# A ring of six one-chunk buffers for r, k, v, shared with w2, and w1 loaded in 12 KB runs

## Chip, cores, metric

One core of one Trainium2 chip. The metric is device microseconds of one execution. The kernel before: 128.2 us, median of 3 runs (128.12 to 129.5). Runs more than 1.5% above the fastest run of the same kernel are called slow; ratios use fast runs alone.

## The reference, cut to what matters

```python
# r, k, v: (4, 8, 768, 48) f32; w, u: (8, 48)
for t in range(S):                                   # linear attention, per batch and head
    cur = einsum('bhd,bhe->bhde', u * k[t], v[t])
    y[t] = einsum('bhd,bhde->bhe', r[t], state + cur)
    state = w * state + einsum('bhd,bhe->bhde', k[t], v[t])
x = y as (3072, 384)
# soft mixture of experts: 8 experts of 4 slots, w1: (8, 384, 1024), w2: (8, 1024, 384) f32
logits = x @ phi
slot_input = softmax(logits, axis=0).T @ x
slot_out[e] = relu(slot_input[e] @ w1[e]) @ w2[e]
out = softmax(logits, axis=1) @ slot_out             # (3072, 384) f32
```

Inputs are 14.2 MB of r, k, v and 25.2 MB of weights. The weights are cast to bf16 on the way in, 12.6 MB written.

## The kernel before, where it matters

The attention runs in 12 chunks of 256 rows (`nS` = 12). r, k, v come through SyncE's hardware queue (q1 in the profile), the weights through GpSimd's software queue (q0). GpSimd also does three multiplies of every chunk but the first. Three terms are used below: the masks are VectorE's multiplies of the attention scores, two groups per iteration; an expert is one 768 KB weight load of w1 or w2; the second down projection is the product with w2 of the last four experts, after which the output follows.

```python
ld = ctx.enter_context(tc.tile_pool(name="ld", bufs=2))      # two buffers of one batch (3 chunks)
SRC = ((1, k), (0, r), (2, v))
def load_part(bt, i):                 # batch 0: chunk by chunk, 384 B reads
    for x, src in SRC:
        nc.sync.dma_start(out=bt[:, x, :, i, :],
                          in_=src[0, :, i * TS:(i + 1) * TS, :].rearrange("h (p j) d -> p h (j d)", j=J))
def load(b):                          # batches 1 to 3: three chunks in one load, built as 1536 B reads
    bt = new_batch(b)
    for x, src in SRC:
        nc.sync.dma_start(out=bt[:, x].rearrange("p h i m -> p (h i) m"),
                          in_=src[b].rearrange("h (i p j) d -> p (h i) (j d)", p=P, j=J))
# ... cut ...
w1_ap = moe_w1.rearrange("e (mo p) f -> p e mo f", p=P)      # three 4 KB runs per partition and expert
# ... cut: mults(n) for n > 0 ...
    nc.gpsimd.tensor_mul(rr[:, :, :, 0:D], r_l, W_n[:])      # waits for r of chunk n
    load_w(inner)                                            # issues weights in between
    nc.gpsimd.tensor_mul(kk[:, :, :, 0:D], k_l, W_k[:])      # waits for k of chunk n
    nc.gpsimd.tensor_mul(ku, ku, u_b)
# ... cut: schedule, experts issued inside mults(n + 3) and at the end of iteration n ...
W_IN = [0, 0, 1, 0, 0, 1, 1, 1, 1]
W_AT = [0, 0, 1, 0, 0, 1, 1, 1, 3, 0, 0]
mults(1); mults(2); load_w(2)
for n in range(nS - 1):
    masks(n, 0)                                              # VectorE, start of iteration n
    if n + 3 < nS: mults(n + 3, W_IN[n])
    # ... cut ...
    if n % nSb == 1: load(n // nSb + 2)                      # next batch, when its buffer is read out
    load_w(W_AT[n])                                          # after n = 8: all the rest
```

The last four experts of w2 go into one batch buffer once r, k, v have left it (`w_tail`).

The softmax here doesn't subtract the row's maximum and nothing guards it: scores larger than these inputs give would overflow.

## Time and profile before

| | before |
|---|---|
| time, span of the profiled run | 128.2 us, 126.4 us |
| last masks (end of the attention's VectorE work) | 92.04 us |
| second down projection waits for w2 until | 104.93 us |
| from there to the end | 21.5 us |

The prediction shows the slices and the chain; three more readings are needed later. First, the page's rows for GpSimd (busy share) and the granted TensorE clock (share of full speed), 40 slices of 3.16 us, in tenths:

```profile
POOL 6009999799999799999999999992420000055100
PEclk9999999999959999977999599958999999995555
```

GpSimd is busy almost without a gap from 10 us to about 84.

Third, all the waits of the list of waits that r, k, v cause (total us, times, longest):

```profile
POOL rr L254 <- DMA rkv<-in_r_dram: 8.7, 3, 6.8
...
ACT v_bf L264 <- DMA rkv<-in_v_dram: 1.8, 1, 1.8
...
DVE rkv L283 <- POOL rkv L257: 1.1, 1, 1.1
```

6.8 of the 8.7 us are the first wait, for the first loads to land.

### The profile page before, as it was taken

The numbers are of one execution on the slowest core, as the hardware profiler recorded it, in microseconds if no ns is written. First come the engines' busy times: TensorE is split into PE (matmuls) and PEld (weight loads), VectorE is DVE, ScalarE is ACT, GpSimd is POOL, SyncE is SP. The second block draws the span as 40 slices with busy tenths as digits, with TensorE's granted clock in tenths as the row PEclk, the third lists the DMA queues.
The fourth block names the chain that finished last, engine by engine and source line by source line (L and its number), as shares of the span: only waits on it lengthen the run. The fifth ranks groups of instructions, "written<-read, shape, count | busy, mean of one in ns | idle before, by whom it ended". The sixth has DMA issues, their size and how long they took to land.

```text
span 126.4 us, 4165 instructions
## 1 busy us (share of the span) xinstructions
PE 97.5 (77%) x1783; PEld 70.5 (56%) x1783; DVE 91.7 (73%) x181; ACT 78.4 (62%) x144; POOL 81.4 (64%) x77
## 2 busy tenths in 40 slices
PE   3994898887599969189798969799999998793000
PEld 3493575665487757177576657677665565520000
DVE  5599989969989999578999798979762411497000
ACT  5869498868479968488597688886431510495000
POOL 6009999799999799999999999992420000055100
PEclk9999999999959999977999599958999999995555
DMA  3999998999999999999999999999999998079992
GB/s 84 299 325 325 335 327 264 321 208 251 265 332 267 235 259 270 340 289 270 258 255 252 226 211 223 221 214 215 210 218 212 218 199 160 2 264 372 381 403 81
DMA packets 23080, 31.78 MB, mean 251 GB/s; under 512 B 10451, under 2 KB 18005, under 8 KB 23061
## 3 DMA queue, kind: packets, MB, share of 16 engines
q0 software_dynamic: 5360, 15.19, 56.7%
q1 hardware_dynamic: 17280, 16.32, 41.8%
q8 instruction: 14, 0.23, 0.7%
q10 hardware_dynamic: 420, 0.00, 0.2%
q14 instruction: 6, 0.04, 0.1%
HBM read 39.38 MB, written 4.72 MB: 349 GB/s over the span
## 4 chain that ended last, share of the span: by engine, by line
POOL 33%; DMA 25%; PE 10%; SPq 9%; DVE 8%; issue 4%; ACT 2%; POOLq 1%; DVEq 0%
DMA w_tail<-in_moe_w_dram 16%; POOL kk L256 10%; POOL rkv L257 9%; DMA rkv<-in_r_dram 8%; SPq L75 7%; POOL rr L254 7%; DVE o_s L748 5%; POOL w_all L187 2%; POOL w_h L194 2%; PE t_p L312 2%; POOL hT L121 1%; SPq L83 1%; PE so_p L681 1%; PE sr_p L712 1%; PE aat_p L331 1%
## 5 line engine op out<-in xcount | busy, mean ns | idle before, releaser
L343 DVE TENSOR_TENSOR at_s<-aat_p,mask 128x512 bf16<-128x512 f32 x47 | 30.2, 684 | 4.0 <-PE aat_p L331 3.8
L254 POOL TENSOR_TENSOR rr<-rkv,W_n 128x768 bf16<-128x768 f32 x11 | 19.9, 1813 | 8.9 <-DMA rkv<-in_r_dram 8.7
L257 POOL TENSOR_TENSOR rkv<-rkv,u_rep 128x768 f32<-128x768 f32 x11 | 19.9, 1812 | 0.9
L256 POOL TENSOR_TENSOR kk<-rkv,W_k 128x768 bf16<-128x768 f32 x11 | 20.0, 1817 | 0.1
L331 PE MATMUL aat_p<-t_rr,t_kk 64*64 64x128 bf16 x376 | 12.1, 243 | 7.8 <-ACT t_kk L319 4.7
L277 ACT COPY rpun<-rkv 128x384 f32<-128x384 f32 x23 | 11.3, 490 | 10.3 <-PE rpun L491 8.2
L331 PEld LDWEIGHTS <-t_kk 64*64 64x64 bf16 x384 | 8.6, 119 | 11.2 <-ACT t_kk L319 6.9
L283 DVE TENSOR_TENSOR rkv<-rkv,rpun 128x384 f32<-128x384 f32 x23 | 12.6, 546 | 1.3 <-POOL rkv L257 1.1
L301 DVE TENSOR_TENSOR dv<-v_bf,rpun 128x768 bf16<-128x768 bf16 x12 | 11.4, 953 | 2.4 <-ACT v_bf L264 1.4
L319 ACT COPY t_kk<-t_p 128x1024 bf16<-128x1024 bf16 x12 | 12.2, 1014 | 1.0 <-PE t_p L312 1.0
L752 POOL DMA_DIRECT2D out_dram<-o_s x1 | 0.6, 552 | 18.4 <-ACT o_s L750 18.4
L294 DVE TENSOR_REDUCE rpun<-rkv 128x16 f32<-128x768 f32 x12 | 11.5, 961 | 0.4
L382 PE MATMUL s_p<-v_bf,kk 64*128 64x96 bf16 x160 | 11.8, 222 | 0.0
L319 ACT COPY t_rr<-t_p 128x1024 bf16<-128x1024 bf16 x11 | 11.2, 1016 | 0.5 <-PE t_p L312 0.3
L391 DVE TENSOR_TENSOR st<-s_p,wm 128x384 bf16<-128x384 f32 x20 | 10.9, 546 | 0.4 <-PE s_p L382 0.4
L264 ACT CAST v_bf<-rkv 128x768 bf16<-128x768 f32 x12 | 10.0, 830 | 1.8 <-DMA rkv<-in_v_dram 1.8
L382 PEld LDWEIGHTS <-kk 64*128 64x128 bf16 x160 | 8.5, 104 | 4.0 <-issue 3.9
L433 ACT COPY xt_s<-xl_p 128x768 bf16<-128x768 bf16 x11 | 8.8, 798 | 1.4 <-PE xl_p L431 1.1
L412 ACT CAST x_t<-y_p 128x384 bf16<-128x384 f32 x22 | 9.6, 495 | 0.0
L488 PE MATMUL rpun<-Lexp,x_t 128*128 128x32 bf16 x66 | 5.1, 179 | 5.2 <-DVE dv L301 5.2
L312 PE MATMUL t_p<-ident,kk 128*128 128x128 bf16 x96 | 8.8, 246 | 0.2 <-ACT t_rr L319 0.2
L312 PE MATMUL t_p<-ident,rr 128*128 128x128 bf16 x88 | 8.5, 253 | 0.0
(132 smaller groups left out, 194.7 us busy)
## 6 DMA issues: line engine op xcount, KB each, us to landing
w_all<-in_moe_w_dram POOLq DMA_DIRECT2D x8, 768.0 KB, 11.6
w_h<-in_moe_w_dram POOLq DMA_DIRECT2D x4, 768.0 KB, 13.2
w_tail<-in_moe_w_dram POOLq DMA_DIRECT2D x3, 768.0 KB, 19.7
out_dram<-o_s POOLq DMA_DIRECT2D x6, 384.0 KB, 6.7
out_dram<-o_s SPq DMA_DIRECT2D x5, 384.0 KB, 6.1
rkv<-in_k_dram SPq DMA_DIRECT2D x3, 384.0 KB, 4.4
rkv<-in_r_dram SPq DMA_DIRECT2D x3, 384.0 KB, 4.6
rkv<-in_v_dram SPq DMA_DIRECT2D x3, 384.0 KB, 5.3
```

Source lines behind the costliest of these rows:

```text
L254: nc.gpsimd.tensor_mul(rr[:, :, :, 0:D], r_l, W_n[:])
L256: nc.gpsimd.tensor_mul(kk[:, :, :, 0:D], k_l, W_k[:])
L257: nc.gpsimd.tensor_mul(ku, ku, u_b)
L277: nc.scalar.copy(rp, loads[n][0][:, j, :, :])
L283: nc.vector.tensor_mul(s["ku"][:, j, :, :], s["ku"][:, j, :, :], s["rps"][j])
L294: nc.vector.tensor_reduce(d, s["ku"], axis=mybir.AxisListType.X, op=ALU.add)
L301: nc.vector.tensor_mul(dv[:], s["v"][:], d[:, :, :, None].to_broadcast([P, J, H, D]))
L312: nc.tensor.transpose(t_p[:, q, :, j, :], s[nm][:, j, 2 * q:2 * q + 2, :].rearrange("p h d -> p (h d)"), ident[:])
L319: nc.scalar.copy(t_s[:], s.pop("p_" + nm)[:])
L331: nc.tensor.matmul(at_p[a][g * HF:(g + 1) * HF, q, :], kT[sl, q, g, j, :], rT[sl, q, g, :, :].rearrange("p j c -> p (j c)"), start=True, s ...
L343: nc.vector.tensor_mul(s["at"][:, a, j, :, :], at_p[a][:], mask[:, j, None, :].to_broadcast([P, nP, P]))
L382: nc.tensor.matmul(s_p[:, q * D2:(q + 1) * D2], s["kk"][sl, j, 2 * q:2 * q + 2, :].rearrange("p h d -> p (h d)"), s["v"][sl, j, 2 * q:2 * ...
```

## The change

The intent: ask for r, k, v earlier, one chunk at a time, as soon as one chunk is read out; move w1 in long runs; let w2's last experts into single ring buffers as these come free.

```diff
-    ld = ctx.enter_context(tc.tile_pool(name="ld", bufs=2))
+    ld = ctx.enter_context(tc.tile_pool(name="ld", bufs=6))
+    NL = 6
+    def load(n):
+        b, i = divmod(n, nSb)
+        bt = ld.tile([P, 3, H, J * D], f32, name="rkv")
+        for x, src in SRC if n == 0 else (SRC[1], SRC[0], SRC[2]):      # r, k, v
+            nc.sync.dma_start(out=bt[:, x],
+                              in_=src[b, :, i * TS:(i + 1) * TS, :].rearrange("h (p j) d -> p h (j d)", j=J))
-    w1_ap = moe_w1.rearrange("e (mo p) f -> p e mo f", p=P)
+    w1_ap = moe_w1.rearrange("e (p mo) f -> p e mo f", p=P)
-        if e == XE and f0 == 0:      (one tail tile for four experts of w2)
+        if e >= XE and f0 == 0:      (one tail tile, one ring buffer, per expert)
-    for f in range(0, nF, 2):        (last expert in four pieces)
+    for f0, f1 in ((0, 4), (4, 6), (6, nF)):
+                x_v = x_of[n][g].rearrange("p (c m) -> p m c", m=nM)
-                    nc.tensor.matmul(..., x_of[n][g][:, mi * P:(mi + 1) * P], le[:, q, :],
+                    nc.tensor.matmul(..., x_v[:, mi, :], le[:, q, :],
-        W_IN = [0, 0, 1, 0, 0, 1, 1, 1, 1]
-        W_AT = [0, 0, 1, 0, 0, 1, 1, 1, 3, 0, 0]
+        W_IN = [0, 0, 1, 0, 1, 1, 1, 1, 1]
+        W_AT = [0, 0, 0, 0, 1, 1, 1, 1, 2, 0, 0]
-        load_w(2)
+        load_w(1)
-            if n % nSb == 1:
-                load(n // nSb + 2)
+            load(n + 1 + NL)
-            put = nc.sync.dma_start if i % 2 == 0 else nc.gpsimd.dma_start
+            put = nc.gpsimd.dma_start if i and i % 2 == 0 else nc.sync.dma_start
-                    (nc.sync if j == 0 else nc.gpsimd).dma_start(out=out_ap[i][:, j, :], in_=o_s[:, j, :])
+                    put(out=out_ap[i][:, j, :], in_=o_s[:, j, :])
```

Cut: the first calls of `load` (chunks 0 to 5 at the start, chunk 6 after the first cast of v), renamed w2 views, the order of two filler groups in the last down projection.

More of the change, by code (lines that the diff above doesn't have):

```diff
@@ L57 @@
     w1_all = wts.tile([P, E, nM, F], bf, name="w1_all")
-    w2_h = [wts.tile([P, E // 2, nF, Dm], bf, name="w2_h")[:]]
+    w2_h = wts.tile([P, E // 2, nF, Dm], bf, name="w2_h")
+    w2_of = [w2_h[:, e] for e in range(E // 2)]
     ident = wts.tile([P, P], bf, name="ident")
-    ld = ctx.enter_context(tc.tile_pool(name="ld", bufs=2))
+    ld = ctx.enter_context(tc.tile_pool(name="ld", bufs=6))
     cst = ctx.enter_context(tc.tile_pool(name="cst", bufs=1))
     loads = {}
+    NL = 6
     SRC = ((1, k), (0, r), (2, v))
-    def new_batch(b):
-        bt = ld.tile([P, 3, H, nSb, J * D], f32, name="rkv")
-        for i in range(nSb):
-            loads[b * nSb + i] = [bt[:, x, :, i, :].rearrange("p h (j d) -> p j h d", j=J) for x in range(3)]
-        return bt
-    def load_part(bt, i):
-        for x, src in SRC:
-            nc.sync.dma_start(out=bt[:, x, :, i, :],
-                              in_=src[0, :, i * TS:(i + 1) * TS, :].rearrange("h (p j) d -> p h (j d)", j=J))
-    def load(b):
-        if b >= B:
-            return
-        bt = new_batch(b)
-        for x, src in SRC:
-            nc.sync.dma_start(out=bt[:, x].rearrange("p h i m -> p (h i) m"),
-                              in_=src[b].rearrange("h (i p j) d -> p (h i) (j d)", p=P, j=J))
-    b_first = new_batch(0)
-    load_part(b_first, 0)
+    def load(n):
+        if n >= nS:
+            return
+        b, i = divmod(n, nSb)
+        bt = ld.tile([P, 3, H, J * D], f32, name="rkv")
+        loads[n] = [bt[:, x].rearrange("p h (j d) -> p j h d", j=J) for x in range(3)]
+        for x, src in SRC if n == 0 else (SRC[1], SRC[0], SRC[2]):
+            nc.sync.dma_start(out=bt[:, x],
+                              in_=src[b, :, i * TS:(i + 1) * TS, :].rearrange("h (p j) d -> p h (j d)", j=J))
+    load(0)
     warm = cst.tile([P, 1], f32, name="warm")
@@ L101 @@
                             in_=w.rearrange("(q a) d -> a d q", a=2)[par])
-    for i in range(1, nSb):
-        load_part(b_first, i)
-    load(1)
+    for n in range(1, NL):
+        load(n)
     row_i = cst.tile([P, 1], mybir.dt.int32, name="row_i")
@@ L189, in w2_load @@
     def w2_load(e, f0=0, f1=nF):
-        if e == XE and f0 == 0:
-            tail = ld.tile([P, (E - XE) * nF * Dm], bf, name="w2_tail", tag="rkv",
-                           padded_shape=[P, 3 * H * nSb * 2 * J * D])
-            w2_h.append(tail[:].rearrange("p (e f d) -> p e f d", e=E - XE, f=nF))
-        nc.gpsimd.dma_start(out=w2_h[e // XE][:, e % XE, f0:f1, :], in_=w2_ap[:, e, f0:f1, :])
+        if e >= XE and f0 == 0:
+            tail = ld.tile([P, nF * Dm], bf, name="w2_tail", tag="rkv", padded_shape=[P, 2 * 3 * H * J * D])
+            w2_of.append(tail[:].rearrange("p (f d) -> p f d", f=nF))
+        nc.gpsimd.dma_start(out=w2_of[e][:, f0:f1, :], in_=w2_ap[:, e, f0:f1, :])
     w_todo = []
@@ L199 @@
     w_todo.pop()
-    for f in range(0, nF, 2):
-        w_todo.append((w2_load, (E - 1, f, f + 2)))
+    for f0, f1 in ((0, 4), (4, 6), (6, nF)):
+        w_todo.append((w2_load, (E - 1, f0, f1)))
     w_todo.reverse()
@@ L486, in disp @@
                 q = 2 * (n % 2) + g
+                x_v = x_of[n][g].rearrange("p (c m) -> p m c", m=nM)
                 for mi in range(nM):
-                    nc.tensor.matmul(un_p[:, mi * ES:(mi + 1) * ES], x_of[n][g][:, mi * P:(mi + 1) * P], le[:, q, :],
+                    nc.tensor.matmul(un_p[:, mi * ES:(mi + 1) * ES], x_v[:, mi, :], le[:, q, :],
                                      start=(n == 0 and g == 0 and mi == 0), stop=(n == nS - 1 and g == 1),
@@ L535 @@
         v_cast(0)
+        load(NL)
         tables()
@@ L681, in down @@
                     nc.tensor.matmul(so_p[c * ES:(c + 1) * ES, :], hT[:, x, fi, c * ES:(c + 1) * ES],
-                                     w2_h[x][:, c, fi, :],
+                                     w2_of[x * XE + c][:, fi, :],
                                      start=(x == 0 and fi == 0), stop=(x == 1 and fi == nF - 1),
@@ L712, in last_down @@
                     nc.tensor.matmul(sr_p[c][:], hL[:, fi, :, :].rearrange("p g t -> p (g t)"),
-                                     w2_h[1][:, XL, fi, c * HD:(c + 1) * HD],
+                                     w2_of[E - 1][:, fi, c * HD:(c + 1) * HD],
                                      start=(fi == 0), stop=(fi == nF - 1), skip_group_check=True)
-        last_down(0, 2)
         keep(2)
-        last_down(2, 4)
+        last_down(0, 4)
         keep(1)
```

## The prediction

> **What bounds the kernel now.** I read the page first (slices, then chain), then the chain in order of time, then the timeline around the points where the chain changes hands. Columns of the slices are 3.16 us each.
>
> ```profile
> span 126.4 us, 4165 instructions
> ...
> DVE  5599989969989999578999798979762411497000
> ...
> DMA  3999998999999999999999999999999998079992
> ...
> DMA w_tail<-in_moe_w_dram 16%; POOL kk L256 10%; POOL rkv L257 9%; DMA rkv<-in_r_dram 8%; SPq L75 7%; POOL rr L254 7%; DVE o_s L748 5%; POOL w_all L187 2%; POOL w_h L194 2%; PE t_p L312 2%; POOL hT L121 1%; SPq L83 1%; PE so_p L681 1%; PE sr_p L712 1%; PE aat_p L331 1%
> ```
>
> The DMA row is full from 3 to about 105 us and again from 111 to 124 us; VectorE is nearly full from 6 to 90 us. So two chains run side by side through the attention stage, and neither has much slack. The timeline shows where they meet:
>
> ```profile
> 103.04 1.15 PE L689 MATMUL pad_f<-w_all,ident 128*128 128x384 bf16 x6
> ...
> 104.12 0.34 PE L681 MATMUL so_p<-w_tail,hT 128*32 128x384 bf16 x2
> ...
> 104.93 1.46 PE L681 MATMUL so_p<-w_tail,hT 128*32 128x384 bf16 x22 [0.47 <-DMA w_tail<-in_moe_w_dram]
> ```
>
> The second down projection could start at 104.12 by the compute chain and got its third expert's w2 at 104.93. From there on 21.5 us follow (last matmuls, then the output at DMA rate), the same in both kernels but for small things. So a speed-up of one chain alone is worth at most 0.8 us; both have to move. GpSimd is long on the printed chain, but only because it issues the weights: it ended the multiplies of the last chunk at 79.8 and VectorE took them at 83.4.
>
> Where the compute chain loses time to data:
>
> ```profile
> 9.73 1.81 POOL L254 TENSOR_TENSOR rr<-rkv,W_n 128x768 bf16<-128x768 f32 x1 [6.81 <-DMA rkv<-in_r_dram]
> 23.02 1.81 POOL L254 TENSOR_TENSOR rr<-rkv,W_n 128x768 bf16<-128x768 f32 x1 [0.87 <-DMA rkv<-in_r_dram]
> 28.52 0.55 DVE L283 TENSOR_TENSOR rkv<-rkv,rpun 128x384 f32<-128x384 f32 x1 [1.11 <-POOL rkv L257]
> 41.98 1.81 POOL L254 TENSOR_TENSOR rr<-rkv,W_n 128x768 bf16<-128x768 f32 x1 [1.07 <-DMA rkv<-in_r_dram]
> 52.33 0.83 ACT L264 CAST v_bf<-rkv 128x768 bf16<-128x768 f32 x1 [1.79 <-DMA rkv<-in_v_dram]
> 53.19 0.95 DVE L301 TENSOR_TENSOR dv<-v_bf,rpun 128x768 bf16<-128x768 bf16 x1 [1.37 <-ACT v_bf L264]
> 54.12 0.42 PE L331 MATMUL aat_p<-t_rr,t_kk 64*64 64x128 bf16 x16 [2.95 <-ACT t_kk L319]
> ```
>
> The third v batch is late at 52.3; PE idles 2.95 us, and the next PE stretch is slow too (granted clock 0.78 from 52 to 58 us). A VectorE iteration with no wait took 6.43 us (19.70 to 26.13); the ones touched by these lines took 7.04 (26.13 to 33.17), 7.75 (46.83 to 54.58) and 7.47 (54.58 to 62.05).
>
> [...] In the queues' view of 44 to 49 us, with w1 (2 KB written per packet) and r, k, v (1.5 KB) both waiting, they go nearly one to one, 348 to 380[...]:
>
> ```profile
> q0 software_dynamic: 348, 0.69, 72.5%
> q1 hardware_dynamic: 380, 0.58, 36.7%
> ```
>
> [...] The dispatch will now load weights with a step of 3 elements (6 bytes). [...] L667 loads with a step of 8 elements (16 bytes) at 150 ns mean, against 98 ns for the contiguous L431. [...]
>
> **The change part by part.** Numbers of the order view and built program: TensorE, VectorE and ScalarE keep their instructions; SP issues 36 loads instead of 18; GpSimd one DMA less in the output.
>
> 1. w1 in 12 KB runs. 8 x 128 x 3 = 3072 packets of 2 KB become 1024 of 6 KB, as w2 has them. While w1 was alone (26 to 29 us) 305 packets took 3 us of 16 engines: 157 ns each, so 3072 cost 30.1 us of the 16 engines. w2's packets follow each other every 455 ns in the trace's records: 1024 cost 29.1 us. Saved: 1.0 us of DMA time. Only that, because 4 KB reads were already near the rate. Issuing drops from 0.80 to 0.60 us, 8 times, so 1.6 us of GpSimd, which has slack.
>
> 2. The ring. Chunk 6 may be fetched once chunk 0 is read (12 us) rather than when all of batch 0 is read (24.9 us). The two holes in the DMA row, at 20.5 to 22 us (about 0.7 us lost) and 54 to 55 us (about 0.5 us), close: 1.1 us of DMA time. Alone, 384 B packets give 313 GB/s (3 to 10 us, first batch), the 1.5 KB ones 330 GB/s (14 to 19 us), of which the first has other small traffic; so cutting the later batches to 384 B costs at most 0.5 us, and I take 0.2.
>
> 3. Order r, k, v and chunk arrival. r of chunk 1 is fourth instead of fifth: 384 KB at 325 GB/s is 1.2 us, so GpSimd starts at 8.5 instead of 9.73. The waits at 23.02 and 41.98 go. Iterations 26.13, 46.83 and 54.58 come down: 0.6 + 1.3 + 0.5 (half of the slow-clock one, an estimate) = 2.4 us.
>
> 4. Strided weights: 72 loads, 6 per iteration[...].
>
> 5. Output: the second half of block 0 goes to SP, and block 1 too; the row after 110 us has one hole of 0.35 us at 111.8 that this fills: 0.3 us. The last expert in 3 pieces instead of 4: nothing, its last use is at 108.
>
> Sum: DMA chain 104.9 - 1.0 - 1.1 + 0.2 = 103.0, at best 102.5 if the engines' skew falls too (w2 of the third expert ended between 101.7 and 103.7 by engine). Compute chain 104.1 - 2.4 + 0.2 = 101.9. The later one sets the end: a gain of 1.9 to 2.4 us there, with 0.3 in the output about 2.5, from a time of 128.2: **125.7 us**. I lean a little below that since the early schedule of the weights is also thinned (one w1 instead of two before 23 us), which frees r, k, v further: **125.5 us**.
>
> **The rivals.**
>
> (a) r, k, v starved by long weight packets. The built program reads 384 B per descriptor in every chunk load, where the old batch loads read 1.5 KB. If packets alternate one to one, r, k, v get 384 B for each 6 KB packet of about 455 ns: 384 x 16 / 477 ns = 13 GB/s while weights queue, against 116 in the window above (0.58 MB in 5 us). For: the 348 to 380 above, and the late v at 52.3 is already that effect. Against: 10 of 12 chunks are fetched by about 48 us, when the weights are few (three before then). Worked through, k of chunk 10 would reach GpSimd at about 73 instead of 66 us; that stall would drain the weights' queue, let chunk 11 through, and delay VectorE by 2 to 4 us: gate 104 to 106, time 126.5 to 129. If v of chunk 11 is caught behind all of w2, 135 us or more.
>
> (b) VectorE is the bound whatever arrives: it is 88% busy from 10 to 94 us (windows of 6 us), and clock dips come in iterations without data waits too (0.80 at 70 to 76, 0.72 at 82 to 88 us). Then compute gains 1 us only, gate 103.1: no worse than the DMA gate, time 126.1.
>
> (c) The loads are hidden and DMA stays the bound with new holes, since weights come later: weights demand two of 3.7 us per 6.6 us from 48 us on, so the queue should not run dry; if it does, each us lost is one us of the end: 126 to 127.
>
> **Range and chances.** Two per cent is 125.6, on my figure. (a) in its mild form has a chance of about a third and gives about "same"; its bad form a tenth. Without it 124 to 126. Range 123.4 to 128.6; faster 0.50, same 0.41, slower 0.09.
>
> **What would show it.** Right: no ScalarE wait on v, no GpSimd wait on r after the first; first multiply at about 8.5; iterations of about 6.5 us before 62; w1 packets of 6 KB at the w2 spacing; no hole at 21 us; second down projection starting at 102 to 103; output stage 0.3 us shorter. Wrong: GpSimd or ScalarE waiting on r, k, v of chunks 9 to 11 between 60 and 90 us with q0 far ahead of q1 in packets times bytes (rival a); weight loads of the dispatch over 110 ns (part 4); the down projection waiting long on w_tail with DMA holes before it (c).

Its sum: 103.0 us for the DMA chain, 101.9 for the compute chain, a time of 125.5 us. One term of it, the + 0.2 us of the compute chain, is part 4, the strided weight loads, the author's estimate. The trace of before has contiguous loads and a step of 8 elements, none of 3.

## More of the kernel before

Second, the page's packets and queues (packets, MB, share of 16 engines):

```profile
DMA packets 23080, 31.78 MB, mean 251 GB/s; under 512 B 10451, under 2 KB 18005, under 8 KB 23061
...
q0 software_dynamic: 5360, 15.19, 56.7%
q1 hardware_dynamic: 17280, 16.32, 41.8%
```

## The result, and the profile after

141.44 us, median of 4 runs (139.86 to 143.17), against 128.85 for the kernel before beside it: a ratio of 1.096, 95% interval 1.083 to 1.108. Slower, where 123.4 to 128.6 us was expected. Ratios are the mean time of one kernel's fast runs over that of the other's in the same rounds, so not quite the ratio of the medians. The profiled run is a fast one (139.86 us, span 138.0). Its page, with the same rows as shown of before, in slices of 3.45 us:

```profile
span 138.0 us, 4185 instructions
...
DVE  6599987999699999599952968805935241189100
...
POOL 6049999999999999910029995059970000005200
PEclk9999999999699999599999555559555999999555
DMA  3999999999999899999999999995999995038993
...
DMA packets 42055, 31.79 MB, mean 230 GB/s; under 512 B 38370, under 2 KB 38884, under 8 KB 42036
...
DMA rkv<-in_k_dram 31%; DMA rkv<-in_r_dram 5%; POOL kk L246 5%; DVE o_s L738 4%; POOL rr L244 4%; DMA w_pd<-in_w_dram 3%; POOL rkv L247 3%; PE t_p L302 2%; PE pad L508 2%; PE s_p L372 2%; PE so_p L672 2%; PE h_p L643 2%; DVE rkv L242 2%; DVE at_s L333 2%; DVE rkv L273 1%
```

GpSimd has two holes, at about 59 to 71 and 85 to 91 us, which it did not have; VectorE has 2 tenths in the slice at 72.5 us and none in that at 90; the granted clock falls to 0.5 behind them; the same bytes go in 42055 packets instead of 23080; and where w_tail led the chain (the work that ended last, followed back from the end) with 16%, k now leads with 31%. Whose wait the holes are shows in the chain in order of time (start, duration, what):

```profile
45.65 25.63 DMA rkv<-in_k_dram
...
71.44 1.79 POOL kk L246
73.59 17.29 DMA rkv<-in_k_dram
...
91.05 1.79 POOL kk L246
```

One 384 KB load takes 25.6 us, another 17.3. GpSimd's timeline (start, duration, instruction, in brackets the idle time before it and what ended it) and VectorE's give what they cost:

```profile
71.42 1.80 POOL L246 TENSOR_TENSOR kk<-rkv,W_k 128x768 bf16<-128x768 f32 x1 [12.35 <-PE aat_p L321]
91.03 1.80 POOL L246 TENSOR_TENSOR kk<-rkv,W_k 128x768 bf16<-128x768 f32 x1 [6.40 <-DMA rkv<-in_k_dram]
```

```profile
75.14 0.56 DVE L273 TENSOR_TENSOR rkv<-rkv,rpun 128x384 f32<-128x384 f32 x1 [4.19 <-POOL rkv L247]
94.74 0.56 DVE L273 TENSOR_TENSOR rkv<-rkv,rpun 128x384 f32<-128x384 f32 x1 [5.17 <-POOL rkv L247]
```

These are k of chunks 9 and 11. The first wait is put down to TensorE by the releaser column, but the chain shows the k load landing at that moment. Why a load takes 25 us is in the queues' view of 56 to 60 us:

```profile
q0 software_dynamic: 147, 0.80, 97.3%
q1 hardware_dynamic: 146, 0.06, 7.8%
```

One packet each in turn, 147 to 146 (the view counts 4 B records too, 16 of the 147); but a weight packet now carries 6 KB and one of r, k, v 384 B. r, k, v get 0.06 MB in 4 us, 15 GB/s, while the weights get 200.

The time, put together: iteration 8 of the attention began at 69.67 us (68.55 before), so 1.1 us had been lost by then. The last masks came at 103.83 us (92.04), so iterations 8 to 11 lost another 10.7: 9.4 are the two VectorE waits above, the rest, 1.3 us, I put down to the clock granted there (0.51 from 76 to 82 us, 0.50 from 82 to 88; before 1.00 and 0.72). The second down projection (TensorE's timeline) started with its weights in place, no idle time before it:

```profile
117.01 1.48 PE L672 MATMUL so_p<-w_tail,hT 128*32 128x384 bf16 x24
```

117.01 us against 104.93, and from there to the end it took 21.0 us (21.5 before).

There is also a small loss at the start, from VectorE's timeline of 7 to 13 us:

```profile
9.04 2.56 DVE L242 TENSOR_TENSOR rkv<-rkv,u_rep 128x768 f32<-128x768 f32 x1
```

This multiply took 0.95 us in the kernel before. r of chunk 1 is now fourth in the queue, GpSimd starts its first multiply at 8.68 us instead of 9.73, and that multiply (2.11 us instead of 1.81) runs beside VectorE's. In the trace these overlapping multiplies all took longer: VectorE's, 2.56 us long, ends at 11.60, that is 0.84 us after GpSimd's next multiply came up at 10.76, and that next one took 2.52 us instead of 1.80. Why they delay each other is not shown. First masks: 13.63 us instead of 12.04.

### The profile page after: what moved, and what is told of

Its sections match the earlier page's. It is cut to its first block, busy times and chain, and to the rows that moved or that the text cites. A ratio compares the mean times of both kernels' runs of the same rounds, so it can differ in the third digit from the quotient of the medians.

```text
span 138.0 us, 4185 instructions
## 1 busy us (share of the span) xinstructions
PE 105.5 (76%) x1783; PEld 76.2 (55%) x1783; DVE 93.6 (68%) x181; ACT 78.7 (57%) x144; POOL 79.0 (57%) x74
## 2 busy tenths in 40 slices
DMA packets 42055, 31.79 MB, mean 230 GB/s; under 512 B 38370, under 2 KB 38884, under 8 KB 42036
## 4 chain that ended last, share of the span: by engine, by line
DMA 39%; PE 24%; DVE 13%; POOL 12%; issue 3%; ACT 1%; ACTq 1%; POOLq 1%; DVEq 0%; SPq 0%
DMA rkv<-in_k_dram 31%; DMA rkv<-in_r_dram 5%; POOL kk L246 5%; DVE o_s L738 4%; POOL rr L244 4%; DMA w_pd<-in_w_dram 3%; POOL rkv L247 3%; PE t_p L302 2%; PE pad L508 2%; PE s_p L372 2%; PE so_p L672 2%; PE h_p L643 2%; DVE rkv L242 2%; DVE at_s L333 2%; DVE rkv L273 1%
## 5 line engine op out<-in xcount | busy, mean ns | idle before, releaser
L246 POOL TENSOR_TENSOR kk<-rkv,W_k 128x768 bf16<-128x768 f32 x11 | 20.7, 1881 | 18.8 <-PE aat_p L321 12.3
L321 PE MATMUL aat_p<-t_rr,t_kk 64*64 64x128 bf16 x376 | 13.3, 265 | 6.8 <-DVE at_s L333 2.7
L744 POOL DMA_DIRECT2D out_dram<-o_s x5 | 2.7, 547 | 23.2 <-DVE o_s L738 22.7
L321 PEld LDWEIGHTS <-t_kk 64*64 64x64 bf16 x384 | 9.4, 133 | 10.3 <-ACT t_kk L309 4.6
L372 PE MATMUL s_p<-v_bf,kk 64*128 64x96 bf16 x160 | 13.2, 239 | 0.0
L372 PEld LDWEIGHTS <-kk 64*128 64x128 bf16 x160 | 9.7, 113 | 4.7 <-issue 4.7
L394 PE MATMUL y_p<-v_bf,at_s 64*128 64x48 bf16 x384 | 8.6, 192 | 4.8 <-DVE at_s L333 4.7
L394 PEld LDWEIGHTS <-at_s 64*128 64x128 bf16 x384 | 6.8, 100 | 7.2 <-DVE at_s L333 5.2
L479 PE MATMUL rpun<-Lexp,x_t 128*128 128x32 bf16 x66 | 5.5, 186 | 5.8 <-DVE dv L291 5.8
```

The source lines that it names most:

```text
L321: nc.tensor.matmul(at_p[a][g * HF:(g + 1) * HF, q, :], kT[sl, q, g, j, :], rT[sl, q, g, :, :].rearrange("p j c -> p (j c)"), start=True, s ...
L372: nc.tensor.matmul(s_p[:, q * D2:(q + 1) * D2], s["kk"][sl, j, 2 * q:2 * q + 2, :].rearrange("p h d -> p (h d)"), s["v"][sl, j, 2 * q:2 * ...
L394: nc.tensor.matmul(s["y"][g][:, h * D:(h + 1) * D], s["at"][sl, a, j, q, :], s["v"][sl, j, h, :], start=False, stop=(a == 1 and q == nP - ...
```

## The experiments

Two theories at the outset. **Starvation**: r, k, v in 384 B packets lose their turns to 6 KB weight packets. **12 KB runs of w1**: it is the longer w1 packets that do it, and the ring is sound. A third came later: **DMA holes**, the weights come too late and the DMA engines stand idle. Times below are medians of all runs; the fast runs are named where the median mixes both kinds.

### One part of the change at a time

**Only the 12 KB runs**, on the kernel before (two batch buffers, 1.5 KB reads):

```diff
-    w1_ap = moe_w1.rearrange("e (mo p) f -> p e mo f", p=P)
+    w1_ap = moe_w1.rearrange("e (p mo) f -> p e mo f", p=P)
+                x_v = ...   (and the strided dispatch weights)
```

> The kernel before with one part alone: w1 in 12 KB runs (and the strided weight loads of the dispatch that go with it). Theory (r, k, v starve because one of their packets goes for one weight packet): here r, k, v keep 1.5 KB packets, so against 6 KB weight packets they get about 1536 x 16 / (78 + 455) ns = 46 GB/s, not 13; in the queues' view the packets go one to one while both wait; total DMA work is 1 us less. Time 126.5 to 129.5, no stall of GpSimd over 3 us. Rival 1 (long weight packets are harmful by themselves): 132 or more. Rival 2 (the strided weight loads slow TensorE): L488-like weight loads over 120 ns at granted clock 1.0 and 1 to 3 us longer with no new data wait.

131.75 us; the fast runs 128.75 and 130.59, before 128.83. In the profiled fast run r of chunk 6 is 7.56 us late, 1.07 us before the change:

```profile
47.99 1.79 POOL L254 TENSOR_TENSOR rr<-rkv,W_n 128x768 bf16<-128x768 f32 x1 [7.56 <-DMA rkv<-in_r_dram]
```

So long weight packets starve even the 1.5 KB reads ("no stall of GpSimd over 3 us" was a miss), but cost 0 to 2 us in the fast runs.

**The change without the 12 KB runs** (w1 again in 4 KB runs, the rest of the change as it is):

```diff
-    w1_ap = moe_w1.rearrange("e (p mo) f -> p e mo f", p=P)
+    w1_ap = moe_w1.rearrange("e (mo p) f -> p e mo f", p=P)
```

> The changed kernel with w1 back in 4 KB runs (2 KB written per packet), all else as changed. Theory: while w1 waits, r, k, v get 384 x 16 / (22 + 157) ns = 34 GB/s instead of 13, so k of chunk 9 comes earlier (the 12.4 us stall of GpSimd shrinks to 3 to 9 us); against w2 (6 KB packets) nothing changes. Time 132 to 139. Rival (the ring or the small descriptors are slow whatever the weights are): no change, 140 to 142. Rival (12 KB runs alone did it): 126 to 130.

143.2 us, ratio 1.102 (1.090 to 1.114). A miss: I expected 132 to 139; it is nearer to the first rival, that the ring or the small reads are slow whatever the weights are. The 12 KB runs are not the main cause. The second theory falls.

**Only the small reads**, on the kernel before: batch loads cut into chunk loads, no ring, 4 KB runs:

```diff
-            nc.sync.dma_start(out=bt[:, x].rearrange("p h i m -> p (h i) m"),
-                              in_=src[b].rearrange("h (i p j) d -> p (h i) (j d)", p=P, j=J))
+            for i in range(nSb):
+                nc.sync.dma_start(out=bt[:, x, :, i, :],
+                                  in_=src[b, :, i * TS:(i + 1) * TS, :].rearrange("h (p j) d -> p h (j d)", j=J))
```

> The kernel before with its batch loads cut into chunk loads of 384 B descriptors; two batch buffers, w1 in 4 KB runs and the schedule of before stay. Theory: alone these packets move as fast, but while weights wait r, k, v get 34 GB/s instead of 116 (13 beside w2): the batches land later, batch 3 worst, since w1 waits from 54 us on without a pause; GpSimd stalls once or twice, 2 to 10 us: time 129 to 138. Rival (only the 12 KB w1 matters): 128 to 129, no new wait.

136.75 us, ratio 1.059 (1.051 to 1.068), a hit. The same bytes into the same buffers in the same order, only in smaller packets (and so three loads issued in place of one), cost 6%, over half of the whole loss. (The profiled run of this kernel was a slow one; I read no difference from it.) How the rest divides between the ring, the earlier pairs of experts and the 12 KB runs, no run isolates.

**Only the output order**, on the kernel before:

```diff
-            put = nc.sync.dma_start if i % 2 == 0 else nc.gpsimd.dma_start
+            put = nc.gpsimd.dma_start if i and i % 2 == 0 else nc.sync.dma_start
-                    (nc.sync if j == 0 else nc.gpsimd).dma_start(...)
+                    put(...)
```

> The kernel before with only the output part of the change (both halves of block 0 and the odd blocks on SyncE's queue, the others on GpSimd's). My prediction gave this 0.3 us: 128.5 against 128.8, so 'same'. The theory that the loss is all in the loads says the same: within 0.5 us either way. Rival (the output order costs): 129.5 or more, with the output stage (last matmul group to the end) longer than 16.2 us.

128.15 us, ratio 0.991 (0.982 to 0.999). In its profile the second down projection was released at 105.77 us and the end came 20.7 us later, against 21.5 before: the output stage is 0.8 us shorter, more than the 0.3 expected. It is the fastest version found, by under 1%, too little to call it faster.

### Turns between queues

**The changed kernel with v on ScalarE's queue.** The first attempt moved all of v and spoilt its own start:

```diff
-            nc.sync.dma_start(out=bt[:, x],
+            (nc.scalar if x == 2 else nc.sync).dma_start(out=bt[:, x],
```

> The changed kernel with v loaded through ScalarE's queue instead of SyncE's, nothing else. Theory[...]: r, k, v now have two turns for each weight packet, so while weights queue they get about 28 GB/s instead of 15, GpSimd's and ScalarE's waits on loads roughly halve, and the time is 131 to 137. Rival (the rate of r, k, v is set by something else than turns, for example by the SyncE queue's own issue or by total bandwidth): the rate stays near 15 GB/s and the time 139 to 143. Rival 2 (v loads issued by ScalarE wait for their buffer and hold ScalarE up): ScalarE shows issue waits of some us, and the gain is lost.

144.7 us. ScalarE's small loads of w and u now stood behind v, and its first logarithm waited 9.8 us; the first masks came at 23.44 us instead of 13.63. The total says nothing on the theory. The second attempt moved only chunks 6 to 11:

```diff
+            (nc.scalar if x == 2 and n >= NL else nc.sync).dma_start(out=bt[:, x],
```

> The test that e7_two_queues spoilt at its start: the changed kernel with v through ScalarE's queue for chunks 6 to 11 only, so that the start is that of the changed kernel (first masks at about 13.6 us). Theory[...]: while weights queue, SyncE's r and k still get about 15 GB/s but share it with no v, so they have a third less to bring in, and v gets 15 GB/s of its own; GpSimd's two long waits (12.35 and 6.40 us) fall by a third to two thirds and the time is 132 to 138. Packets of the two hardware queues and the weights stand near 1 : 1 : 1 while all have work. Rival (the turns are shared between all hardware queues together, or the loads are slow for another reason): waits and time as in the changed kernel, 139 to 143.

138.26 us, and 133.04 in its one fast run. The profiled run is a slow one, so I read from it only the turns, here of 68 to 76 us (q10 is ScalarE's queue):

```profile
q0 software_dynamic: 278, 1.51, 91.3%
q1 hardware_dynamic: 278, 0.11, 7.3%
q10 hardware_dynamic: 270, 0.10, 4.7%
```

One to one to one: here a second queue took a second turn, 278 : 278 : 270. The fast run lies 8 us under the changed kernel's median, inside the 132 to 138 expected, though one fast run is thin; all four runs (133.04 to 138.96) lie under the changed kernel's fastest, 139.86. That GpSimd's waits on k fall was expected too and is not shown: they were 18.0 us in this slow run, against 18.75 in the changed kernel's fast one.

### The transfers alone

Three kernels with no compute at all (wrong result): w1 through GpSimd's queue, r, k, v through SyncE's, each to its own place.

```diff
+    for e in range(E):
+        nc.gpsimd.dma_start(out=w1_all[:, e, :, :], in_=w1_ap[:, e, :, :])
+    for b in range(B):
+        for x, src in ((0, r), (1, k), (2, v)):      # m1: chunk loads; m2, m3: batch loads
+            nc.sync.dma_start(...)
```

> Not the kernel: only its transfers, no compute (the result is wrong on purpose). All eight experts of w1 in 12 KB runs are issued by GpSimd at the start, all of r, k, v as 384 B chunk loads (r, k, v in order, batch by batch) by SyncE, each to its own place. Measures the disputed DMA cost by itself. Theory (turns, one packet each): until the weights are in, packets stand 1:1 and r, k, v get about 15 GB/s; 64 weight packets per engine at 475 + 20 ns make 32 us, then the other 2240 small packets per engine at 19.6 ns make 44 us: last r, k, v landing at about 78 us (2 us of start included). Rival (turns are not taken one to one when nothing else runs): r, k, v get over 50 GB/s in the first 30 us.

> As m1_384_12k, but r, k, v in batch loads of three chunks, 1536 B reads. While weights last, r, k, v get four times the rate of m1_384_12k, about 58 GB/s. Last landing: by the rates of the two sizes alone (313 and 330 GB/s) 2.3 us before m1_384_12k for 14.2 MB; by the fit of packet counts to full stretches of the kernels' traces (20.5 against 73.8 ns a packet) 4.6 us before it. Whichever it is, three quarters of that is what the ring costs the changed kernel in DMA time, where the prediction took 0.2 us.

> As m2_1536_12k, but w1 in 4 KB runs (2 KB written per packet) as before the change. The prediction gave the long runs 1.0 us of DMA time: then this one lands 1.0 us later than m2_1536_12k. By the fit (3072 packets at 157 ns against 1024 at 475 ns) the two are equal within 0.3 us. While weights last, r, k, v should get about 105 GB/s.

The queues of 10 to 30 us, for m1, m2 and m3:

```profile
q0 software_dynamic: 735, 4.02, 97.0%
q1 hardware_dynamic: 735, 0.28, 7.6%
```

```profile
q0 software_dynamic: 668, 3.69, 88.9%
q1 hardware_dynamic: 665, 1.00, 15.7%
```

```profile
q0 software_dynamic: 1459, 2.86, 75.2%
q1 hardware_dynamic: 1460, 2.21, 35.0%
```

The turns are exact (4 B records counted, 80 of the 735 of m1's q0), and what r, k, v get follows the two packet sizes: 0.28, 1.00 and 2.21 MB in 20 us, so 14, 50 and 110 GB/s. That settles the starvation. Alone, once the weights were in, the 384 B packets ran at 321 GB/s (m1, 40 to 60 us) and the 1.5 KB ones at 326 (m2, 45 to 65 us).

The totals settle the other question. By the packet records, from the first packet to the last of r, k, v took 74.6 us (m1), 73.0 (m2) and 73.7 (m3); the times were 80.48, 79.77 and 80.25. So for all 14.2 MB small reads cost 0.7 us by the times and 1.6 by the packet records (m1 against m2), 0.5 to 1.2 for the three batches that the change made small; the 12 KB runs save 0.5 to 0.7 us (m3 against m2). My fit of packet counts, 4.6 us, was wrong.

### Taking the starvation away

**Fewer weights queued while r, k, v are still to come**, on the changed kernel:

```diff
-        W_IN = [0, 0, 1, 0, 1, 1, 1, 1, 1]
-        W_AT = [0, 0, 0, 0, 1, 1, 1, 1, 2, 0, 0]
+        W_IN = [0, 0, 1, 0, 1, 1, 1, 1, 2]
+        W_AT = [0, 0, 0, 0, 0, 0, 0, 2, 2, 0, 0]
```

> The changed kernel with only the schedule of the weight issues altered: 6 instead of 9 weight transfers issued before GpSimd takes r of chunk 11, the others right after. Same descriptors, same ring. Theory: r, k, v arrive in time, no GpSimd stall over 3 us after the first chunk, VectorE loses no 10 us; the weights end at 105 to 107 us, the second down projection starts at 102 to 106 us: time 125 to 130. Rival (384 B descriptors or the ring cost time by themselves): still 135 or more.

143.04 us; one fast run, 136.5. A miss: 125 to 130 expected. The profiled run was slow, 147.53 us, and its trace says why that run was: ScalarE waited 19.0 us for v of chunk 11, last in its queue and caught behind w2.

**The same, with k last**, so that GpSimd's own wait for k holds the next weights back until v is in; chunk 1 again as k, r, v:

```diff
-        for x, src in SRC if n == 0 else (SRC[1], SRC[0], SRC[2]):
+        for x, src in SRC if n <= 1 else (SRC[1], SRC[2], SRC[0]):      # r, v, k
```

> The thinned schedule of e3_thin, plus the load order: k, r, v for chunks 0 and 1, and r, v, k (k last) for chunks 2 to 11. Theory (in e3_thin the v of chunk 11 was last in its queue, so GpSimd went on to queue all of w2 once r and k were in, and v crawled in behind it at one 384 B packet per 6 KB one): with k last, GpSimd's own wait for k means that v has landed before more weights are queued, so the ScalarE wait on v of chunk 11 (19.0 us in e3_thin) goes to under 1 us, and the time is 126 to 132. GpSimd/VectorE collision theory: with r of chunk 1 fifth again, GpSimd starts at about 9.7 us, the VectorE multiply by u of chunk 0 takes 0.95 us instead of 2.56, and the first masks start near 12.0 instead of 13.6 us. Rival (the short packets are too slow in themselves, whatever is queued): the time stays above 136, with the wait moved to GpSimd's k.

136.23 us, three runs of four within 0.13 us of each other, ratio 1.058 (1.050 to 1.067). The time is a miss, 126 to 132 expected; the waits did as expected. No wait on v at all, and on k 3.7 us in two. The start is repaired: VectorE's multiply takes 0.95 us and the first masks stand at 12.04. The attention is now faster than in the kernel before: last masks at 89.32 us instead of 92.04. But the second down projection waits for w2, on TensorE's timeline:

```profile
107.19 0.48 PE L672 MATMUL so_p<-w_tail,hT 128*32 128x384 bf16 x1 [3.31 <-DMA w_tail<-in_moe_w_dram]
110.85 2.72 PE L672 MATMUL so_p<-w_tail,hT 128*32 128x384 bf16 x22 [3.18 <-DMA w_tail<-in_moe_w_dram]
```

110.85 us instead of 104.93. Neither theory had this: the end moved from the compute chain to the DMA chain. By 80 us all of r, k, v were in here and before, but 1.4 MB less had been moved in all (GB/s of the windows 4 to 35, 35 to 60 and 60 to 80 us: 266, 254, 242 against 292, 282, 236). At the 215 GB/s of the last stretch that is 6.4 us of weights, about the 5.9 seen.

**Are those 5.9 us holes?** One is plain in the DMA row of 30 to 34 us, 0.1 us a digit, of e5_thin_order and then of before:

```profile
DMA  5211011000000023666479999999998943944996
```

```profile
DMA  7989999899979899797989999799999989999998
```

Most are not, since records overlap: the row's share reads 1.16 when 384 B packets alone keep it full (m1) and 1.04 when 6 KB packets do. So I priced each packet by m1 to m3 and the trace of before, and took what a stretch of 2 us did not use as idle. In 16 engines times 5 us m1 moves some 162 pairs of a 6 KB and a 384 B packet (about 490 ns a pair), m2 150 pairs with 1.5 KB (about 530 ns), m3 350 pairs of 2 KB and 1.5 KB (about 230 ns). Alone a packet costs 19.1 ns (384 B), 75.2 (1.5 KB), 157 (2 KB) and 455 (6 KB). By these prices the stretches of m1 and m2 come out full. Idle DMA time between 4 and 104 us, all from fast profiles:

| kernel | idle, of it before 35 us | last masks | second down projection released |
|---|---|---|---|
| before | 1.4 us, 0.6 | 92.04 | 104.93 |
| changed | 8.0 us, 2.2 | 103.83 | 117.01 (weights in place) |
| e5_thin_order | 6.5 us, 4.1 | 89.32 | 110.85 |
| e9_even | 5.3 us, 2.6 | 95.89 | 110.51 |
| e12_early | 6.5 us, 1.5 | 98.38 | 112.52 |

e5_thin_order lost 5.1 us more to holes than the kernel before, and its w2 came 5.9 us later. This is an accounting that I worked out, not a counter. A recount with the same prices came out 0.7 to 1.3 us higher for each kernel, with the same 5.1 between these two. Without prices, the time in which fewer than 16 records are open (what is missing from 16, a lower bound) is 0.8 us before, 3.6 in e5_thin_order, 4.5 in the changed kernel, and only 1.5 in e9_even and 2.3 in e12_early: so over half of e5_thin_order's holes are seen in the records, while those of the last two rest on the prices.

**Weights spread evenly**, and **more of them early**, to fill the holes, both with the loads ordered as in e5_thin_order:

```diff
-        W_IN = [0, 0, 1, 0, 1, 1, 1, 1, 2]
-        W_AT = [0, 0, 0, 0, 0, 0, 0, 2, 2, 0, 0]
+        W_IN = [0, 1, 1, 1, 1, 1, 1, 1, 1]        (e9_even)
+        W_AT = [0, 0, 0, 0, 0, 0, 0, 1, 1, 0, 0]
+        W_IN = [1, 1, 0, 1, 1, 1, 0, 1, 1]; load_w(2)      (e12_early, W_AT as e9_even)
```

> e5_thin_order (k last) with the weights spread evenly: one expert inside each of iterations 1 to 8, none withheld early, so the DMA hole of e5_thin_order at 20 to 32 us (share 0.89 where full stretches show 1.05, about 1.9 us lost) closes. Theory (with starvation gone, DMA time is the bound, and the 384 B packets cost about 3.5 us of it more than the 1.5 KB ones by a fit of packet counts to full stretches): the second down projection starts at 108 to 109.5 instead of 110.8, the time is 133 to 135.5, still 4 to 5% over the kernel before, with no wait on r, k, v over 2 us after the first. Rival (e5_thin_order lost only through its hole): 130 or less. Rival 2 (starvation comes back with more weights queued early): GpSimd waits on k of 5 us and more, time 137 or more.

> e9_even (k last, thinned) with more weights before 35 us: two experts at the start instead of one and one inside iterations 0 and 1, none inside iterations 2 and 6. By the packet costs that m1 to m3 gave, the DMA engines stood idle between 4 and 104 us for 1.4 us in the kernel before, 8.0 in the changed kernel, 6.5 in e5_thin_order and 5.3 in e9_even, of which 2.9 lie before 35 us. Theory (what is left after starvation is holes, since the ring asks for r, k, v one chunk at a time and weights come too late to fill them): holes before 35 us fall to about 1 us, the second down projection starts at 108 to 109, the time is 131 to 133. Rival (starvation returns with the early weights): GpSimd waits on k for 4 us or more before 35 us, and the time is 134 or more.

e9_even: 135.55 us; fast runs 133.59 and 133.99. Those are in the expected range, but the release at 110.51 is not the 108 to 109.5 expected, and starvation is partly back: GpSimd waits on k four times, 8.0 us in all, and the last masks stand at 95.89 instead of 89.32. e12_early: 135.43 us, ratio 1.051 (1.044 to 1.059). 131 to 133 expected; here the rival won. The early holes did fill (2.6 to 1.5 us), but starvation came back, after 35 us and not before it as the rival had said:

```profile
43.26 1.80 POOL L246 TENSOR_TENSOR kk<-rkv,W_k 128x768 bf16<-128x768 f32 x1 [7.59 <-DMA rkv<-in_k_dram]
```

And since GpSimd issues no weights while it waits, new holes opened behind it, by the accounting. So the two losses are coupled: more weights early starved k (7.59 us in e12_early), fewer left the DMA engines idle (4.1 us before 35 us in e5_thin_order, by the accounting).

### Two attempts at a better kernel

Both on the kernel before with the output order of e6_output; the second without 12 KB runs:

```diff
-        W_AT = [0, 0, 1, 0, 0, 1, 1, 1, 3, 0, 0]
+        W_AT = [0, 0, 0, 0, 0, 1, 2, 1, 3, 0, 0]
+    w1_ap = moe_w1.rearrange("e (p mo) f -> p e mo f", p=P)      (e8_mix only)
```

> An attempt at a better kernel: the kernel before (two batch buffers, 1.5 KB reads) with w1 in 12 KB runs, the output order of the change, and one expert of w1 taken from the end of iteration 2 and given to iteration 6, so that fewer long packets queue against the third batch. Theory (starvation of r, k, v is what made e1_w1_runs 131.75): GpSimd's wait for r of chunk 6 (7.56 us in e1_w1_runs) falls under 2 us and the time is 126.5 to 129. If it stays at 130 or more, 12 KB runs cost in another way, or the fourth batch is caught instead.

133.04 us, one fast run of 129.33. A miss: 126.5 to 129 expected. Its profiled run was slow, so the trace tells no more.

> An attempt at a better kernel: e6_output (the kernel before with the changed output order) with one expert of w1 moved from the end of iteration 2 to the end of iteration 6. Theory (queued weights are what makes r of chunk 6 and v of chunk 6 late even in the kernel before: 1.07 us of GpSimd at 41.98, 1.79 us of ScalarE at 52.3): both waits go; DMA time sets the end, so the gain is at most some tenths: 127 to 128.3. Rival (the weight that comes later opens a DMA hole before 46 us): each us of hole adds one to the end, 128.5 to 130.5.

130.13 us, ratio 1.010 (1.005 to 1.015), six fast runs. A miss, 127 to 128.3 expected. The rival won: an expert of w1 moved from iteration 2 to 6 makes the end later, w2 released the down projection at 105.87 us (3.3 us of waiting for it). Other schedules of the kernel before were not tried.

## Why the prediction was wrong

**Where the kernel was bound: right.** Two chains side by side with 0.8 us between them. The experiments bear it out: e5_thin_order shortened one by 2.7 us and lengthened the other by 5.9.

**The step that failed is the use of rival (a).** The mechanism and its rate were there: 13 GB/s predicted, 15 measured. What failed is the argument "Against: 10 of 12 chunks are fetched by about 48 us, when the weights are few". By 47 us packets for nine chunks had moved, not ten; k of the tenth, chunk 9, was issued at 45.65 us and landed at 71.3. The diff starts the pairs of experts (one inside an iteration, one at its end) at iteration 4, where before they start at 5, so five experts were issued between 45.25 and 58.50 us, some 18 us of turns at 15 GB/s. Then: "that stall would drain the weights' queue, let chunk 11 through". It did drain, but GpSimd, set free at 71 us, issued the next weights before k of chunk 11 was in, and stalled again. The 2 to 4 us of VectorE became 9.4, plus a granted clock of 0.5 from 76 to 88 us. The form of "135 or more" that I gave a tenth was tied to v of chunk 11; it came by k of chunks 9 and 11 instead. r, k, v need 1.18 MB per iteration of 6.5 us, 181 GB/s; a rival that leaves them a twelfth of that deserved more than a third.

**Part 1, the 12 KB runs:** 1.0 us of DMA time predicted, 0.5 to 0.7 measured (m2 against m3). Right in kind. Not foreseen in its own part: they more than halve what r, k, v get (50 against 110 GB/s with 1.5 KB reads), which cost e1_w1_runs 7.56 us of GpSimd waiting.

**Part 2, the ring:** wrong. The two holes that would "close: 1.1 us of DMA time" became 1.4 us of holes before and 8.0 after by the accounting. The hole at 20 us stayed, 0.57 us in both. Small reads: 0.2 us taken, 0.5 to 1.2 measured. This was a slip of my own: 10.6 MB at 313 and at 330 GB/s differ by 1.7 us, not "at most 0.5".

**Part 3, chunk arrival:** right on what it gives when r, k, v arrive: e5_thin_order brought the last masks 2.7 us forward, 2.4 predicted. The sum is partly luck: the three iterations named gave 1.1, 1.7 and -0.4 us there and in the changed kernel alike, against 0.6, 1.3 and 0.5. The waits named did go: no ScalarE wait on v, no wait on r after the first. Wrong on r of chunk 1: GpSimd's start came 1.05 us earlier (1.2 predicted) and cost 1.6 us of VectorE, whose multiply beside it took 2.56 us instead of 0.95.

**Part 4, strided weights:** small, as estimated. The median L479 load, with its step of 3 elements, took 104 ns against 96 before (the mean, 107, has some of up to 148 ns in it), so 72 of them 0.6 us.

**Part 5, output:** right in kind, 0.5 us in the changed kernel and 0.8 in e6_output against 0.3.

**Rival (b), VectorE as the bound:** not borne out. It allowed the compute chain 1 us; e5_thin_order gained 2.7.

**Rival (c), holes because weights come later:** held to be about a us. By the accounting it is 5.1 of the 5.9 us that e5_thin_order lost, and 2.8 of them show in the records. It could not be seen in the changed kernel's time, since starvation came first. That holes set the end rests in part on the accounting in e5_thin_order and wholly on it in e9_even; no run filled them without bringing starvation back, so it is not shown by intervention. Also open: how often v of chunk 11 is caught in e3_thin, as only a slow run was profiled.

## What to carry to other kernels

Two streams on the same DMA engines shared them by packet, not by byte (735 to 735, 14 against 201 GB/s): before cutting one stream's loads smaller or making the other's packets longer, divide the two packet sizes and ask whether the smaller stream can live on that fraction for as long as the other one is queued. An engine that issues transfers and also waits for others, as GpSimd here, couples the two: its stall stops the issue (no weights for the 12.35 us in which it waited for k of chunk 9), and a hole can come back later. And in a kernel balanced between two chains, check each schedule change on both ends; a gain of 2.7 us on one was worth nothing here.
